# Laying x and v out by piece on the host for the products u = x·v of a long convolution

## Chip, cores and metric

The kernel runs on one core of one Trainium2 chip. The metric is the device time of one execution in microseconds (us); lower is better. Three runs of the kernel before gave a median of 2274.79 us (2274.72 to 2276.05).

## Reference

Two parts follow one another. The first is a long convolution with a gate, for 2 batches of 12480 positions and 128 channels; the second is a dense MLP with a rational function as its activation, over all 24960 positions.

```python
def _attn_ref(x, v, pos_emb, w1, w2):
    B, S, D = x.shape                       # 2, 12480, 128
    h_mlp = np.maximum(pos_emb @ w1, 0.0) @ w2
    window = np.exp(-0.01 * np.arange(S, dtype=np.float32))[:, None]
    h_filt = h_mlp * window
    u = x * v
    L = 2 * S
    Uf = np.fft.rfft(u, n=L, axis=1)
    Hf = np.fft.rfft(h_filt, n=L, axis=0)
    y = np.fft.irfft(Uf * Hf[None, :, :], n=L, axis=1)[:, :S, :]
    return x * y

def _moe_ref(x, w_in, w_out, a, b):         # w_in 128 x 2048, w_out 2048 x 128
    h = x @ w_in
    P = a[0] + a[1] * h + a[2] * h * h + a[3] * h * h * h
    Q = 1.0 + np.abs(b[0]) * np.abs(h) + np.abs(b[1]) * h * h
    return (P / (Q + 1e-06)) @ w_out
```

## The kernel before

The convolution is a Fourier transform in two stages. A position is written as n = 128·m + t: m is the row (98 of them, on the partitions), t the residue (128 of them, in the free dimension). The product u = x·v is therefore kept as tiles of 98 partitions × 32 channels × 128 residues, one for each quarter of the channels; 12480 positions are 97.5 rows of 128, so for residues from 64 on the last row lies behind the end of the sequence and must be zero.

**How u is made.** u comes in pieces: one quarter of the channels (32) by 16 residues. There are 32 pieces a batch. `load_quarter` (L235) loads one piece of x and one of v, through `load_rows` (L133): the tile is 98 partitions × 16 residues × 32 channels, and in DRAM a run of 32 channels is 128 bytes. For residues below 64 that is one transfer for x (L141, 98 rows) and one for v; from 64 on it is two each, 96 full rows (L143) and the short end (L146 for v, with padding; L148 for x). All are issued on SP's queue. `quarter` (L243) makes the tile of u and has POOL set the last two partitions of its upper half to zero (L245). `mult_quarter` (L248) multiplies a piece; it writes u through a turned view, so that neighbouring elements of the output lie 128 floats apart.

**First part** (to about 372 us): the filter's MLP (L494 to L527, 16 tiles in turn), with the weights of the second part converted beside it (`weights_gen`, L450, which loads raw at L323 and L325); then the filter stage from about 82 us on, a loop over 32 groups of four channels in which the transforms of the filter and of batch 0 run: PE (L156, L581, L191 to L194, L588), VectorE (L569 to L577, L174, L175, L206, L207), POOL (L180, L181, L209, L210, L599, L600) and ScalarE. Batch 0's pieces belong to this part, two loaded ahead (`load_u`, L301). Its first eight products run on POOL during the filter's MLP (L559); the other 24 run on VectorE, one in each of the first 24 groups (L641); groups without a product take a step of `weights_gen` instead.

**Second part** (from about 372 us): the MLP, as 208 steps over 52 tiles of positions; L876 to L878 are its first product on PE, L886, L910, L938, L954 and L959 its ScalarE work, L920, L965 and L970 VectorE's, L975 and L981 POOL's, L993 the second product on PE. A list of names with offsets (`FIRST`, `REST`) fixes the order of the instructions on every queue. Into each step go three slots (`slot`, L1021); a slot calls `load_step` (L722) and then takes a piece of the convolution of batch 1 (`conv_step`, L752) or of the inverse transform (L822, L828, L841). `load_step` multiplies on POOL the pieces that have been loaded and issues up to three loads ahead on SP: two products a slot while the first quarter is missing, then one a step. A quarter's products are let in when the transform has come near it. Behind the loads on the same SP queue stand hg (the filter's spectrum for two channels, L709, waited for by VectorE at L202), xt, gt and yc for the inverse transform (L143, L803, L785) and the stores of the output (L1015), in the order of the program; so a load that waits for its buffer holds back what is queued behind it.

Of the kernel before, what the change touches and what calls it, by code (L numbers as in the profile page):

```python
# [9 lines left out]
F32 = mybir.dt.float32  # L10
# [3 lines left out]
ALU = mybir.AluOpType  # L14
# [3 lines left out]
B, S, D = 2, 12480, 128  # L18
FO = 64
DFF = 2048  # L20
N2 = 128
M = 98
# [13 lines left out]
UQ = 32  # L36
UC = 16
NF = DFF // 128
NPT = 5
H2 = N2 // 2  # L40
# [23 lines left out]
def constants():  # L64
    t = np.arange(N2)
    hp = np.arange(N2 // 2)
    m = np.arange(M)
    k1 = np.arange(K1)
    k2 = np.arange(N2)
    f = lambda a: np.ascontiguousarray(a, dtype=np.float32)  # L70
    turn = lambda a, n: 2 * np.pi * (a % n) / n

    def twiddles(ph):
        return f(np.stack([np.concatenate([np.cos(ph)] * 2, 1), np.concatenate([np.sin(ph)] * 2, 1)], 1))

    th = turn(m[:, None] * k1[None, :], N1)
    f1 = f(np.concatenate([np.cos(th), -np.sin(th)], 1))
    tw = twiddles(turn(t[:, None] * k1[None, :], L))

    twh = twiddles(np.tile(turn((2 * hp[:, None] + 1) * k1[None, :], 2 * L), (2, 1)))  # L80
    ps = turn(t[:, None] * k2[None, :], N2)
    dft = f(np.stack([np.cos(ps), np.sin(ps), -np.sin(ps)], 1))
    ph = turn((2 * hp[:, None] + 1) * k2[None, :], 2 * N2)
    ch, sh = np.cos(ph), np.sin(ph)
    dfth = f(np.stack([np.concatenate([ch, sh], 0), np.concatenate([ch, -sh], 0)], 1))
    c, s = ch.T, sh.T
    idfth = f(np.stack([np.concatenate([c, s], 1), np.concatenate([s, c], 1)], 1))
    w = np.where(k1 == 0, 1.0, 2.0) / L
    n2 = np.concatenate([2 * hp + 1, -2 * hp - 1])
    sg = np.where(n2 > 0, 1.0, -1.0)  # L90
    ga = turn(k1[:, None, None] * (2 * N2 * m[None, None, :] + n2[None, :, None]), 2 * L)
    w = w[:, None, None]
    g = f(np.stack([np.cos(ga) * w, -np.sin(ga) * w * sg[None, :, None]], 2))
    win = np.zeros((M * N2,), np.float32)
    win[:S] = WINDOW
    win = win.reshape(M, N2)[:96]
    return {
        "f1": f1,
        "tw": tw,
        "twh": twh,  # L100
        "dft": dft,
        "dfth": dfth,
        "idfth": idfth,
        "g": g,
        "win": f(win),
        "ident": np.eye(128, dtype=np.float32),
    }


@with_exitstack  # L110
def build(ctx: ExitStack, tc, x, v, pos_emb, w1, w2, w_in, w_out, moe_a, moe_b,
          f1_d, tw_d, twh_d, dft_d, dfth_d, idfth_d, g_d, win_d, ident_d, out):
    nc = tc.nc
    ctx.enter_context(tc.manual_schedule())
# [13 lines left out]
    def rows(src, r0, n, t0, k, c0, c):  # L128

        w = src.shape[1]  # L130
        return bass.AP(src.tensor, src.offset + (r0 * N2 + t0) * w + c0, [[N2 * w, n], [w, k], [1, c]])

    def load_rows(dst, src, t0, k, c0, c, pad, queue=nc.sync):  # L133


        h = N2 // 2
        if t0 < h < t0 + k:
            load_rows(dst[:, 0:h - t0], src, t0, h - t0, c0, c, pad, queue)
            load_rows(dst[:, h - t0:k], src, h, t0 + k - h, c0, c, pad, queue)
        elif t0 < h:  # L140
            queue.dma_start(out=dst[0:M], in_=rows(src, 0, M, t0, k, c0, c))  # L141
        else:
            queue.dma_start(out=dst[0:96], in_=rows(src, 0, 96, t0, k, c0, c))  # L143
            if pad:
                a = rows(src, 96, 1, t0, k, c0, c)
                queue.dma_start(out=dst[96:98], in_=bass.AP(a.tensor, a.offset, [[0, 2]] + [list(p) for p in a.ap[1:]]))  # L146
            else:
                queue.dma_start(out=dst[96:97], in_=rows(src, 96, 1, t0, k, c0, c))  # L148

    xb = [x[b] for b in range(B)]  # L150
    vb = [v[b] for b in range(B)]


    def s1_mm(cvt, u, cl0, n, k=M):
# [78 lines left out]
        return pool.tile([K1, 2, N2, CY], F32, tag="ys", name="ys", bufs=1)  # L233

    def load_quarter(pool, b, q, n0, bufs):  # L235
        c0 = q * UQ
        xt = pool.tile([M, UC, UQ], F32, tag="xq", name="xq", bufs=bufs)
        vt = pool.tile([M, UC, UQ], F32, tag="vq", name="vq", bufs=bufs)
        load_rows(xt, xb[b], n0, UC, c0, UQ, False)
        load_rows(vt, vb[b], n0, UC, c0, UQ, True)  # L240
        return xt, vt

    def quarter(pool, name, bufs):  # L243
        u = pool.tile([M, UQ, N2], F32, tag=name[:2], name=name, bufs=bufs)
        nc.gpsimd.memset(u[96:98, :, H2:], 0.0)  # L245
        return u

    def mult_quarter(engine, u, n0, xt, vt):  # L248
        k = M if n0 < H2 else M - 1
        engine.tensor_tensor(  # L250
            out=u[0:k, :, n0:n0 + UC].rearrange("p c t -> p t c"), in0=xt[0:k], in1=vt[0:k], op=ALU.mult)


    wpool = ctx.enter_context(tc.tile_pool(name="wpool", bufs=1))
# [8 lines left out]
    with ExitStack() as st:  # L263
# [30 lines left out]
        for i in range(2):  # L294
            nc.scalar.dma_start(out=bdw2[64 * i:64 * i + 64, :].rearrange("p (s c) -> p s c", s=2),
                              in_=w2.unsqueeze(1).to_broadcast([FO, 2, D]))
# [4 lines left out]
        def load_u():  # L301
            if uload and len(uw) < 2:
                q, n0 = uload.pop(0)
                uw.append((q, n0) + load_quarter(sp, 0, q, n0, 2))

        def mult_u(engine):
            if uw:
                q, n0, xt, vt = uw.pop(0)
                if q not in us:
                    us[q] = quarter(sp, f"hu{q}", 6)  # L310
                mult_quarter(engine, us[q], n0, xt, vt)

        def cvs():
            return spp.tile([128, 2, 512], F32, tag="s", name="cs")
# [290 lines left out]
        for g in range(NG + 3):  # L605
            a = g
            if a < NG:
                zh[a] = ctile(sp, "zh", 2, CG)
                t = cvs()
                s1_mm(t, hf[a // gq], a % gq * CG, CG, MF)  # L610
                s1h_out(t, zh[a])
            a = g - 1
            if 0 <= a < NG:
                hgs[a] = ctile(sp, "hg", 2, CG)
                t = cvs()
# [4 lines left out]
                t = cvs()  # L620
                s1_mm(t, us[a // gq], a % gq * CG, CG)
                s1_out(sp, t, zu[a], CG)
            a = g - 2
            if 0 <= a < NG:
                yy[a] = ctile(sp, "yy", 2, CG)
                t = cvs()
                s2_mm(t, zu.pop(a), CG)
                s2_prod(sp, t, hgs.pop(a), yy[a], CG)
            a = g - 3
            if 0 <= a < NG:  # L630
                if a % 2 == 0:
                    ysd[a // 2] = ystile(sp)
                t = cvs()
                s3p_mm(t, yy.pop(a))
                s3p_out(t, ysd[a // 2], a % 2 * CG, (nc.gpsimd, nc.gpsimd if a < NG - 3 else nc.vector))
                if a % 2 == 1:
                    t = ysd.pop(a // 2)
# [14 lines left out]
    def second_part(short):  # L652
# [69 lines left out]
        def load_step(k=0):  # L722
            for p in us:
                p[2] += p[1] == 0
            for _ in range(2 if not us or us[0][1] else int(k == 0)):
                if coming and (coming[0][0] - 1) * (UQ // CS) <= s1_done[0]:
                    q, n0, xt, vt = coming.pop(0)
                    if q == len(us):
                        us.append([quarter(up, f"uq{q}", 2), N2 // UC, 0])
                    mult_quarter(nc.gpsimd, us[q][0], n0, xt, vt)  # L730
                    us[q][1] -= 1
            while pieces and len(coming) < 3:
                q, n0 = pieces.pop(0)
                coming.append((q, n0) + load_quarter(up, 1, q, n0, 3))
# [345 lines left out]
_INS = ["x", "v", "pos_emb", "w1", "w2", "moe_w_in", "moe_w_out", "moe_a", "moe_b"]  # L1080
_OUTS = [((B * S, D), "float32")]


# [20 lines left out]
```

## Time and profile before

| what | before |
|---|---|
| median of 3 runs | 2274.79 us |
| the profiled execution's own time | 2275.51 us |
| its span in the profile | 2273.6 us |
| PE matmul, PE weight load | busy 89%, 77% |
| VectorE (DVE) | busy 92% |
| ScalarE (ACT) | busy 85% |
| GpSimd (POOL) | busy 90% |
| granted clock of TensorE, mean | 0.981 of full speed |
| DMA packets | 357841, 150.26 MB; under 512 bytes 292518 |
| SP's DMA queue | 124.10 MB, 26.3% of 16 engines' span |

The shares are means over the span; the stages differ, so they tell little of what a change in one stage is worth. The time of the execution is 1.9 us longer than the span. In a timeline a line has the start and the duration in us, the engine, the line of the code, the operation, output and inputs with their sizes, and in brackets how long the engine was idle before and which instruction it had waited for. DVE is VectorE, ACT ScalarE, POOL GpSimd; SPq is SP's instruction queue, on which transfers are issued.

### The profile page before, as it was taken

The page shows a single profiled execution, that of the slowest core. Times are in us where ns is not written, and L with a number is a line of the kernel's source. Part 1 is how long each engine was busy: PE and PEld are TensorE (multiplying, and loading weights), DVE is VectorE, ACT ScalarE, POOL GpSimd, SP SyncE. Part 2 cuts the span into 40 slices and gives each one's busy share as a digit, 9 for nine tenths or more (in the row PEclk, how much of TensorE's full clock was granted, in tenths as well). Part 3 has the DMA queues.
Part 4 walks back from the last instruction along what each step waited for, and adds up shares of the span by engine and source line. Part 5 has one row for each costly group of instructions (what it writes and reads, how often), then busy time and mean ns, then how long its engine had stood idle before and what let it go on. Part 6 is the DMA issues. An engine that isn't in the chain of part 4 may idle for free.

```text
span 2273.6 us, 35833 instructions
## 1 busy us (share of the span) xinstructions
PE 2026.0 (89%) x13344; PEld 1758.5 (77%) x13344; DVE 2083.5 (92%) x2374; ACT 1942.7 (85%) x1971; POOL 2037.5 (90%) x1613
## 2 busy tenths in 40 slices
PE   6899977799999999999999889888888898888887
PEld 3677766688888888888888777777777777777775
DVE  6899995899989997999999889999999999999996
ACT  5422223899989998999999989999999999999996
POOL 4588755999999999899999789999999999999997
PEclk8999998999999999999999999999999999999999
DMA  7456426752155133232122112212112111221100
GB/s 148 113 127 147 117 77 126 118 105 59 46 95 110 43 68 86 62 78 73 53 66 66 46 35 46 42 38 46 32 32 52 31 40 39 48 47 32 36 10 11
DMA packets 357841, 150.26 MB, mean 66 GB/s; under 512 B 292518, under 2 KB 339880, under 8 KB 354776
## 3 DMA queue, kind: packets, MB, share of 16 engines
q1 hardware_dynamic: 350632, 124.10, 26.3%
q10 hardware_dynamic: 7024, 23.76, 3.3%
q8 instruction: 107, 1.75, 0.3%
q14 instruction: 78, 0.64, 0.1%
HBM read 99.65 MB, written 48.17 MB: 65 GB/s over the span
## 4 chain that ended last, share of the span: by engine, by line
POOL 36%; ACT 25%; PE 22%; DVE 10%; issue 3%; DMA 2%; SPq 2%; POOLq 0%; DVEq 0%; ACTq 0%
POOL v L981 19%; POOL v L975 9%; PE acc L993 6%; ACT v L910 6%; ACT l L954 5%; ACT r L959 5%; ACT q L886 4%; POOL q L949 4%; ACT q L938 3%; POOL q L948 2%; PE cv L822 2%; PE cs L588 2%; PE cs L156 2%; PE h L876 2%; PE h L877 2%
## 5 line engine op out<-in xcount | busy, mean ns | idle before, releaser
L981 POOL TENSOR_TENSOR v<-v,q 128x980 f32<-128x980 f32 (+1 forms) x416 | 941.3, 2263 | 49.1 <-DVE q L970 45.7
L993 PE MATMUL acc<-wout,v 128*128 128x128 f32 (+2 forms) x6656 | 843.5, 279 | 113.8 <-POOL v L981 109.0
L993 PEld LDWEIGHTS acc<-wout,v 128*128 128x128 f32 (+2 forms) x6656 | 774.3, 186 | 193.7 <-POOL v L981 168.4
L920 DVE SCALAR_TENSOR_TENSOR v<-v,sc,h 128x980 f32<-128x980 f32 (+1 forms) x416 | 504.7, 1213 | 35.1 <-ACT q L886 29.7
L965 DVE SCALAR_TENSOR_TENSOR q<-q,sc,r 128x980 f32<-128x980 f32 (+1 forms) x416 | 504.6, 1213 | 34.3 <-ACT r L959 33.6
L970 DVE SCALAR_TENSOR_TENSOR q<-q,r 128x980 f32<-128x980 f32 (+1 forms) x416 | 482.0, 1159 | 13.5
L910 ACT ACTIVATE v<-h,sc 128x980 f32<-128x980 f32 (+1 forms) x416 | 438.5, 1084 | 31.6 <-PE h L878 30.3
L959 ACT ACTIVATE r<-l 128x980 f32<-128x980 f32 (+1 forms) x416 | 417.0, 1002 | 9.7 <-DVE q L970 8.9
L975 POOL TENSOR_SCALAR v<-v,sc 128x980 f32<-128x980 f32 (+3 forms) x321 | 422.7, 1317 | 0.0
L954 ACT ACTIVATE l<-q,sc 128x1960 f32<-128x1960 f32 (+1 forms) x208 | 401.3, 1929 | 0.9 <-POOL q L949 0.7
L876 PE MATMUL h<-ahi,win_l 128*128 128x490 f32 (+1 forms) x832 | 360.6, 433 | 29.7 <-DVE v L920 27.2
L877 PE MATMUL h<-alo,win_h 128*128 128x490 f32 (+1 forms) x832 | 319.5, 384 | 0.0
L878 PE MATMUL h<-ahi,win_h 128*128 128x490 f32 (+1 forms) x832 | 317.4, 382 | 0.0
L886 ACT ACTIVATE q<-h 128x980 f32<-128x980 f32 (+1 forms) x303 | 302.6, 999 | 8.9 <-PE h L878 6.2
L876 PEld LDWEIGHTS h<-ahi,win_l 128*128 128x128 f32 x832 | 158.0, 190 | 61.5 <-DVE v L920 37.9
L938 ACT ACTIVATE q<-q,sc 128x1960 f32<-128x1960 f32 (+1 forms) x95 | 185.8, 1955 | 0.0
L878 PEld LDWEIGHTS h<-ahi,win_h 128*128 128x128 f32 x832 | 157.9, 190 | 26.2
L943 ACT ACTIVATE q<-q,sc 128x1470 f32<-128x1470 f32 (+1 forms) x113 | 170.9, 1513 | 0.0
L877 PEld LDWEIGHTS h<-alo,win_h 128*128 128x128 f32 x832 | 158.8, 191 | 13.5 <-DVE alo L847 0.4
L822 PE MATMUL cv<-yc,gt 90*98 90x128 f32 x1004 | 128.2, 274 | 1.5 <-DVE an L828 1.2
L822 PEld LDWEIGHTS cv<-yc,gt 90*98 90x98 f32 x1004 | 118.9, 165 | 13.1 <-DVE an L828 7.5
L949 POOL TENSOR_TENSOR q<-q 128x490 f32<-128x490 f32 (+1 forms) x113 | 111.4, 986 | 9.4
(115 smaller groups left out, 2658.9 us busy)
## 6 DMA issues: line engine op xcount, KB each, us to landing
yc<-y_d SPq DMA_DIRECT2D x23, 900.0 KB
gt<-in_g_dram SPq DMA_DIRECT2D x48, 344.5 KB
h_d<-hg ACTq DMA_DIRECT2D x32, 360.0 KB
y_d<-ys ACTq DMA_DIRECT2D x16, 720.0 KB
hg<-h_d SPq DMA_DIRECT2D x64, 180.0 KB
y_d<-ys SPq DMA_DIRECT2D x16, 720.0 KB
xq<-in_x_dram SPq DMA_DIRECT2D x32, 196.0 KB
vq<-in_v_dram SPq DMA_DIRECT2D x32, 196.0 KB
```

What stands on the lines that cost most here:

```text
L876: nc.tensor.matmul(out=t[:, k, 0:w], lhsT=wl, rhs=hi[:, 0:w], start=True, stop=False)
L877: nc.tensor.matmul(out=t[:, k, 0:w], lhsT=wh, rhs=lo[:, 0:w], start=False, stop=False)
L878: nc.tensor.matmul(out=t[:, k, 0:w], lhsT=wh, rhs=hi[:, 0:w], start=False, stop=True)
L910: nc.scalar.activation(out=v, in_=st_h[s, i], func=AF.Square, bias=col("s"))
L920: stt(out=v, in0=v, scalar=col("k"), in1=h, op0=ALU.add, op1=ALU.mult)
L954: nc.scalar.activation(out=part(st_l, s, i), in_=part(st_q, s, i), func=AF.Ln, **({"bias": col("ka")} if short else {}))
L959: nc.scalar.activation(out=t[:, :, 0:w], in_=halves(st_l[s], i, w), func=AF.Exp, scale=-1.0)
L965: nc.vector.scalar_tensor_tensor(out=q, in0=q, scalar=col("ka") if short else 0.0, in1=st_r[s, i], op0=ALU.add, op1=ALU.mult)
L970: nc.vector.scalar_tensor_tensor(out=q, in0=q, scalar=2.0, in1=st_r.pop((s, i)), op0=ALU.subtract, op1=ALU.mult)
L975: nc.gpsimd.tensor_scalar(out=v, in0=v, scalar1=col("p0" if short else "a0"), scalar2=1.0, op0=ALU.add, op1=ALU.mult)
L981: nc.gpsimd.tensor_tensor(out=v, in0=v, in1=halves(st_q[s], i, w), op=ALU.mult)
L993: nc.tensor.matmul(out=acc[j][0:k, q // 128, :], lhsT=g[:, i, q:q + k], rhs=wout[:, f, :], start=(f == 0 and q == 0), stop=(f == NF - 1), ...
```

## The change

On the host x and v are laid out again, as arrays x_q and v_q with the shape batch, quarter, piece, 98 rows, 32 channels, 16 residues; positions behind the end are zeros. A piece is then contiguous, 98 rows of 2,048 bytes. x itself is still handed over as well, for the gate. The kernel loads a piece of x and one of v with one transfer each; the tiles in SBUF have the channels outside and the residues inside, as u has; the product covers all 98 partitions without a turned view; and the two partitions of u are not set to zero any more. Which engine multiplies, in which order, and how many pieces are loaded ahead stay as they were.

```diff
--- before.py
+++ after.py
@@ -108,7 +108,7 @@
 
 
 @with_exitstack
-def build(ctx: ExitStack, tc, x, v, pos_emb, w1, w2, w_in, w_out, moe_a, moe_b,
+def build(ctx: ExitStack, tc, x, x_q, v_q, pos_emb, w1, w2, w_in, w_out, moe_a, moe_b,
           f1_d, tw_d, twh_d, dft_d, dfth_d, idfth_d, g_d, win_d, ident_d, out):
     nc = tc.nc
     ctx.enter_context(tc.manual_schedule())
@@ -148,7 +148,6 @@
                 queue.dma_start(out=dst[96:97], in_=rows(src, 96, 1, t0, k, c0, c))
 
     xb = [x[b] for b in range(B)]
-    vb = [v[b] for b in range(B)]
 
 
     def s1_mm(cvt, u, cl0, n, k=M):
@@ -233,22 +232,17 @@
         return pool.tile([K1, 2, N2, CY], F32, tag="ys", name="ys", bufs=1)
 
     def load_quarter(pool, b, q, n0, bufs):
-        c0 = q * UQ
-        xt = pool.tile([M, UC, UQ], F32, tag="xq", name="xq", bufs=bufs)
-        vt = pool.tile([M, UC, UQ], F32, tag="vq", name="vq", bufs=bufs)
-        load_rows(xt, xb[b], n0, UC, c0, UQ, False)
-        load_rows(vt, vb[b], n0, UC, c0, UQ, True)
+        xt = pool.tile([M, UQ, UC], F32, tag="xq", name="xq", bufs=bufs)
+        vt = pool.tile([M, UQ, UC], F32, tag="vq", name="vq", bufs=bufs)
+        nc.sync.dma_start(out=xt, in_=x_q[b, q, n0 // UC])
+        nc.sync.dma_start(out=vt, in_=v_q[b, q, n0 // UC])
         return xt, vt
 
     def quarter(pool, name, bufs):
-        u = pool.tile([M, UQ, N2], F32, tag=name[:2], name=name, bufs=bufs)
-        nc.gpsimd.memset(u[96:98, :, H2:], 0.0)
-        return u
+        return pool.tile([M, UQ, N2], F32, tag=name[:2], name=name, bufs=bufs)
 
     def mult_quarter(engine, u, n0, xt, vt):
-        k = M if n0 < H2 else M - 1
-        engine.tensor_tensor(
-            out=u[0:k, :, n0:n0 + UC].rearrange("p c t -> p t c"), in0=xt[0:k], in1=vt[0:k], op=ALU.mult)
+        engine.tensor_tensor(out=u[:, :, n0:n0 + UC], in0=xt, in1=vt, op=ALU.mult)
 
 
     wpool = ctx.enter_context(tc.tile_pool(name="wpool", bufs=1))
@@ -1081,13 +1075,21 @@
 _OUTS = [((B * S, D), "float32")]
 
 
+def by_quarter(x):
+    a = np.zeros((B, M * N2, D), np.float32)
+    a[:, :S] = x
+    a = a.reshape(B, M, N2 // UC, UC, D // UQ, UQ)
+    return a.transpose(0, 4, 2, 1, 5, 3)
+
+
 def kernel(**inputs):
     import concourse.bacc as _bacc
     from concourse.bass_utils import run_bass_kernel_spmd as _run
 
     nc = _bacc.Bacc("TRN2", target_bir_lowering=False, num_devices=1)
     arrays, args = {}, []
-    feeds = [(n, inputs[n]) for n in _INS] + list(constants().items())
+    feeds = [("x", inputs["x"]), ("x_q", by_quarter(inputs["x"])), ("v_q", by_quarter(inputs["v"]))]
+    feeds += [(n, inputs[n]) for n in _INS[2:]] + list(constants().items())
     for name, a in feeds:
         a = np.ascontiguousarray(a)
         if a.dtype == np.float64:
```

## Rows read from the trace of the kernel before

**Rows 1.** The page's first line.

```profile
span 2273.6 us, 35833 instructions
```

**Rows 2.** Windows: us; PE, PEld, DVE, ACT, POOL busy (count); clock, DMA share, GB/s.

```profile
101.25:275.00 173.75, 166.63 (x922) 134.08 (x923) 171.50 (x234) 42.11 (x74) 139.99 (x129) 1.00 0.58 134
330.00:370.00 40.00, 36.14 (x205) 28.73 (x203) 29.40 (x40) 10.92 (x21) 31.04 (x31) 1.00 0.34 108
390.00:420.00 30.00, 17.35 (x99) 14.94 (x98) 19.87 (x19) 23.70 (x22) 23.95 (x15) 0.83 1.07 153
520.00:625.50 105.50, 101.04 (x719) 93.11 (x718) 99.72 (x101) 105.33 (x98) 99.60 (x86) 1.00 0.24 56
625.50:701.40 75.90, 69.87 (x474) 63.80 (x473) 65.26 (x67) 69.20 (x64) 73.27 (x60) 0.96 0.49 94
831.80:904.30 72.50, 66.23 (x453) 58.74 (x452) 59.80 (x65) 62.09 (x64) 71.48 (x65) 0.98 0.48 99
```

**Rows 3.** Timeline of the filter stage with its products: start, us, engine, line, tiles.

```profile
83.31 1.80 POOL L245 MEMSET hu<- 2x2048 f32 x1
...
86.33 1.04 DVE L250 TENSOR_TENSOR hu<-xq,vq 98x512 f32<-98x512 f32 x1
...
199.36 1.11 DVE L250 TENSOR_TENSOR hu<-xq,vq 97x512 f32<-97x512 f32 x1
...
207.53 1.12 DVE L250 TENSOR_TENSOR hu<-xq,vq 97x512 f32<-97x512 f32 x1
```

**Rows 4.** Timeline, VectorE, the same stage once the products are through.

```profile
334.71 0.91 DVE L174 TENSOR_TENSOR ta<-cs,tw 128x720 f32<-128x720 f32 x1
...
338.58 0.91 DVE L569 TENSOR_TENSOR tb<-cs,twh 128x720 f32<-128x720 f32 x1 [0.52 <-POOL zu L181]
...
342.54 0.91 DVE L174 TENSOR_TENSOR ta<-cs,tw 128x720 f32<-128x720 f32 x1
```

**Rows 5.** Waits from 0 to 82 us: us in total, times, longest.

```profile
DVE pw L486 <- DMA pos<-in_pos_emb_dram: 4.3, 3, 2.6
...
DVE i L336 <- DMA raw<-in_moe_w_in_dram: 1.5, 3, 0.8
```

**Rows 6.** Waits from 371 to 440 us, then ScalarE's timeline there.

```profile
POOL uq L250 <- DMA vq<-in_v_dram: 20.9, 6, 13.9
...
413.17 0.99 ACT L886 ACTIVATE q<-h 128x980 f32<-128x980 f32 x1 [2.70 <-POOL v L981]
...
418.64 1.00 ACT L886 ACTIVATE q<-h 128x980 f32<-128x980 f32 x1 [3.60 <-PE h L878]
```

**Rows 7.** Timeline, third and fourth quarter: SP's issues, VectorE's waits behind them.

```profile
640.40 0.33 SPq L803 DMA_DIRECT2D gt<-in_g_dram  x1
...
651.77 1.54 SPq L143 DMA_DIRECT2D xq<-in_x_dram  x1
...
657.01 0.39 SPq L709 DMA_DIRECT2D hg<-h_d  x1
...
660.01 0.91 DVE L202 TENSOR_TENSOR ta<-cv,hg 128x720 f32<-128x720 f32 x1 [4.89 <-DMA hg<-h_d]
...
857.43 0.91 DVE L202 TENSOR_TENSOR ta<-cv,hg 128x720 f32<-128x720 f32 x1 [4.83 <-DMA hg<-h_d]
```

**Rows 8.** Timeline, VectorE in the first microseconds: 256 elements, one element.

```profile
4.28 0.42 DVE L486 TENSOR_TENSOR pw<-pos,ta 82x256 f32<-82x256 f32 x1 [4.28 <-DMA ta<-in_win_dram]
...
10.29 0.16 DVE L370 TENSOR_TENSOR sc<-sc 128x1 f32<-128x1 f32 x1
```

**Rows 9.** Lines by form, POOL, whole span: count, busy us, mean ns, idle before.

```profile
L981 POOL TENSOR_TENSOR v<-v,q 128x980 f32<-128x980 f32 x384 | 881.7, 2297 | 41.9 <-DVE q L970 38.5 <-ACT q L938 3.4
...
L250 POOL TENSOR_TENSOR uq<-xq,vq 98x512 f32<-98x512 f32 x16 | 20.8, 1298 | 17.2 <-DMA vq<-in_v_dram 16.9
...
L245 POOL MEMSET uq<- 2x2048 f32 x4 | 7.2, 1800 | 0.2
```

**Rows 10.** Timeline, POOL, its longest product.

```profile
34.46 3.15 POOL L250 TENSOR_TENSOR hu<-xq,vq 97x512 f32<-97x512 f32 x1
```

## Prediction

> **What bounds the kernel now.** I read the page first, then the windows stage by stage, then the chain of waits and the timelines of the stretches in which x and v are loaded. Of the 2273.6 us of span [rows 1] the loads and products for u lie in the first 905 us; what comes after neither loads nor multiplies them and only moves earlier or later as a whole, because every queue's order is fixed by the program. So the question is which wait ends last in five stretches.
>
> From 101 to 275 us (the filter stage of batch 0) VectorE is busy 171.5 of 173.75 us, POOL 140.0 [rows 2]: VectorE sets the pace. One group of four channels takes 207.53 − 199.36 = 8.17 us while each group carries a product [rows 3], and 342.54 − 334.71 = 7.83 us when the products are through; there VectorE waits 0.52 us before L569 [rows 4]. So without its product VectorE isn't the bound any more: 7.83 us is the floor that other work (PE is busy 36.1 of 40 us there, [rows 2]) sets. Before 82 us VectorE sits idle 4.3 us for pos and 1.5 us for raw [rows 5], transfers that SP issues behind those of x and v. At the start of the second part, POOL waits 20.9 us in six waits for v; ScalarE then stands 2.70 and 3.60 us [rows 6]. In quarters three and four of batch 1 POOL is busy 73.3 of 75.9 and 71.5 of 72.5 us, while the steps between them, without products, are ScalarE's (105.3 of 105.5 us) [rows 2]. In each of the two there is one late filter spectrum: VectorE waits 4.89 and 4.83 us for hg [rows 7], and SP had issued hg only after the four transfers of a piece.
>
> **Part by part.**
>
> *Transfers.* A piece of x and v is now 2 × 98 × 16 rows of 128 bytes, afterwards 2 × 98 rows of 2,048 bytes, with the same 401 kB. From 390 to 420 us, when almost nothing else is moved, the queue shows 153 GB/s at a DMA share of 1.07, so 143 GB/s at a full share; from 330 to 370 us, with rows of some kilobytes, 108 GB/s at 0.34, so 318 [rows 2]. Estimate from these: 2.8 us of all DMA engines a piece now, 1.3 afterwards. Nothing of it is a term by itself; it counts only where somebody waits, below.
>
> *Issues.* SP issues two transfers a piece while n0 < 64 and four above; afterwards always two. One plain issue takes 0.33 us (gt), and the four at 651.77 us, with SP's wait in the first, kept hg back until 657.01 [rows 7]. Two of 0.33 would let hg go some 3.7 us earlier.
>
> *Before 82 us.* Ceiling: the 4.3 + 1.5 us that VectorE waits for pos and raw [rows 5]. Floor: 0, since a pos load waits also for one of three buffers, which VectorE itself frees. I take 3.5, above the middle, because both queues (SP's and the DMA engines') get lighter.
>
> *Products on VectorE (24 of them).* They write u with a step of 512 bytes between neighbours now, afterwards in runs of 16. The first, at 86.33 us, ran with POOL idle (its memset from 83.31 ended at 85.11) and still took 1.04 us; later ones take 1.11 [rows 3]. What would a dense one cost? 256 elements from two SBUF tensors took 0.42 us and one element 0.16 [rows 8]: 0.16 + 511 × 0.26 / 255 = 0.68 us, an estimate. The Trainium skill ("SBUF — State Buffer", section "Door 1: The DMA port swizzle") says that accesses run at full rate while they stay in one 16-byte line and pay at each crossing; by it a step of 512 bytes pays at every element and a run of 16 at every fourth. The trace agrees so far as 1.04 against 0.68 goes. So a product shrinks by 1.11 − 0.68 = 0.43 us; a period of 8.17 − 0.43 = 7.74 lies under the floor of 7.83, so 0.34 a group is what can be had. 24 groups carry one, the first two while the pipeline fills: 22 × 0.34 = 7.5; I take 7.2, because a product still waits a little where POOL is reading. Bounds: 0, and 24 × 0.36 = 8.6.
>
> *Memsets.* Eight of 1.80 us on POOL [rows 9]. The first part's four lie in POOL's slack (34 us between 101 and 275, [rows 2]); if that slack were gone, they'd be 1.8 each. The first one of the second part lies in POOL's wait for v. The other three stand in the POOL-bound bursts and count below.
>
> *Products on POOL.* 32 in the second part, 1298 ns each for 512 elements with the 512-byte step; dense work of POOL's, 980 elements in 2297 ns [rows 9], gives 1200 ns for 512 in proportion. So the step costs POOL 0.1 us at most; I take no change, bounds −0.1 and, upward, the rival below.
>
> *Start of the second part and second quarter.* The first and longest wait (13.9 of the 20.9 us) is covered: POOL's first work on the MLP needs PE, ScalarE and VectorE to go first. What reaches the path is ScalarE's idle time, 2.70 + 3.60 = 6.3 us [rows 6], and one memset of 1.8: ceiling 8.1. I take 5.5; floor 3, if a transfer (yc and gt go first on SP) stays late. Next late there is PE, whose granted clock is 0.83 of its upper level of 2.4 GHz in this stretch [rows 2].
>
> *Third quarter.* The memset's 1.8, and POOL's idle 75.9 − 73.3 = 2.6 that hg caused: 4.4 if POOL then has no idle time at all. I take 4.0; bounds 1.8, and 1.8 + 4.89 = 6.7 if VectorE's whole wait was on the path. *Fourth quarter:* 1.8 + 1.0 = 2.8, I take 2.5, bounds 1.0 and 1.8 + 4.83 = 6.6.
>
> *Sum:* 3.5 + 7.2 + 5.5 + 4.0 + 2.5 = 22.7 us. The profiled execution took 2275.5 us, so 2252.8; the median of the runs is 0.7 below it, so **2252 us**. All floors together give 5.8 (2269 us), all ceilings 35.8 (2239 us).
>
> **Rivals.**
>
> *The products on VectorE don't shrink* (0.16). If what lengthens them is POOL reading SBUF beside them, the layout helps nothing; the sum loses 7.2: 2259 us. For it: they lie between POOL's L181 and L209, and the longer ones exceed the first by 0.07 us. Against it: the first one with POOL idle is almost as long [rows 3]. The Trainium skill (same page, section "Who interferes with whom") has a VectorE instruction with two SBUF inputs contend with a POOL instruction that reads SBUF, which the product is before and after; no row here shows the product dense.
>
> *The loads' waits move instead of going* (0.12). hg also stands behind stores of the output, and the first pieces behind yc. Then 7.2 for VectorE and three memsets of 1.8 remain: 12.6, so 2262 us.
>
> *The transfers aren't what the change says* (0.04): if rows are cut smaller on the way, say to the 64 bytes of one channel, SP and VectorE gain and the DMA engines lose; about 2275 us.
>
> *Slower* (0.03). POOL's product becomes longer, being cut into 32 short rows. The longest product in the trace is one of 3.15 us [rows 10]; 32 × 1.85 = 59 us on an engine that is the bound in the bursts, less 22.7: 2311 us. It decides from 22.7 / 32 = 0.7 us a product upward. Against it: products now write 16 rows of 32 with the largest step and show no cost from it [rows 9].
>
> The forecast itself keeps 0.65.
>
> **How the numbers follow.** 0.2% (4.5 us) is about what can be told from no change here. The forecast and the first two rivals, 0.93 together, lie below 2270; I give 0.02 of that back for several floors at once. Faster 0.91, same 0.05, slower 0.04. The range goes from 2240, near all ceilings, to 2264, past the rival of the loads.
>
> **What the changed profile would show.** Right: xq and vq 64 issues each, 196 kB, none of 2 or 4 kB; L250 on VectorE near 0.7 us, groups 7.8 to 7.9 us apart; no memset of u; hg's waits of 4.8 us gone from VectorE; ScalarE without its two gaps of 2.7 and 3.6 us; POOL's products at 1.3 us; the end 20 us earlier and everything after 905 us of the same length. Wrong: L250 on VectorE still at 1.0 us, or groups stay at 8.17 us because another instruction waits; POOL's wait for v in the second part still 15 us and ScalarE's idle time still there; POOL's product above 2 us.

## The result, and the profile after

The changed kernel took 2254.58 us (median of 5 runs, 2252.79 to 2255.84) beside 2274.79 us for the kernel before in the same series; the ratio is 0.991, with a 95% interval of 0.9899 to 0.992. The interval lies below 1: the kernel is faster by 20.2 us (0.9%), and it ends 2.6 us above the predicted 2252. The profiled execution took 2255.12 us. From the page of the kernel after; the first line answers to [rows 1]:

```profile
span 2253.2 us, 35705 instructions
...
PE 2023.2 (90%) x13344; PEld 1758.5 (78%) x13344; DVE 2073.7 (92%) x2374; ACT 1941.2 (86%) x1971; POOL 2021.5 (90%) x1605
...
DMA packets 169487, 150.31 MB, mean 67 GB/s; under 512 B 91622, under 2 KB 138984, under 8 KB 166424
...
q1 hardware_dynamic: 162280, 124.17, 22.5%
```

The bytes are the same, the packets fewer by half. SP's queue held the DMA engines for 26.3% of 2273.6 us before and 22.5% of 2253.2 now: 598 − 507 = 91 us less, 1.4 us for each of the 64 pieces, about the difference of the prediction's estimates, 2.8 − 1.3.

To see where the time went I cut both traces at the same instructions: VectorE's first of the filter stage (L569 before, L563 after), the second part's first matmul (PE, y and gt), POOL's last product of the second, third and fourth quarters, and VectorE's last copy of a result (128 partitions) for the output, each by its start.

| stage | before, us | after, us | gain | predicted |
|---|---|---|---|---|
| up to the filter stage | 82.36 | 79.55 | 2.8 | 3.5 |
| filter stage | 289.76 | 282.65 | 7.1 | 7.2 |
| start of the second part, second quarter | 110.68 | 106.68 | 4.0 | 5.5 |
| third quarter | 217.34 | 212.42 | 4.9 | 4.0 |
| fourth quarter | 202.91 | 199.76 | 3.2 | 2.5 |
| from there to the last copy | 1361.95 | 1364.04 | −2.1 | 0 |

The first five make 22.0 of the 22.7 us forecast. Then 2.1 us are given back in the part that neither loads nor multiplies x and v.

Windows of the kernel after, with the columns of [rows 2]: the filter stage, the start of the second part, then the product bursts of the third and fourth quarters.

```profile
95.75:266.00 170.25, 168.65 (x937) 136.31 (x936) 167.97 (x238) 42.29 (x74) 133.72 (x129) 1.00 0.43 137
380.00:410.00 30.00, 20.78 (x116) 18.55 (x114) 21.99 (x22) 27.52 (x25) 25.86 (x16) 0.83 0.64 160
...
609.00:683.00 74.00, 70.78 (x506) 64.69 (x505) 68.73 (x70) 73.38 (x68) 73.79 (x61) 1.00 0.37 97
810.90:882.40 71.50, 67.59 (x470) 59.56 (x469) 62.02 (x67) 64.41 (x66) 71.50 (x65) 1.00 0.38 100
```

In the filter stage PE and VectorE are now both within 2.3 us of full. At the start the DMA share is 0.64 where it was 1.07. In the third quarter POOL is idle for 0.2 us where it was idle for 2.6.

Timeline of the kernel after; VectorE's products answer to [rows 3], POOL's L180 is the instruction beside the product, the wait for PE to [rows 6], SP's issues and VectorE's use of hg to [rows 7].

```profile
83.51 0.69 DVE L245 TENSOR_TENSOR hu<-xq,vq 98x512 f32<-98x512 f32 x1
...
199.57 0.83 POOL L180 TENSOR_TENSOR zu<-ta,tb 128x360 f32<-128x360 f32 x1
...
200.20 0.75 DVE L245 TENSOR_TENSOR hu<-xq,vq 98x512 f32<-98x512 f32 x1
...
208.09 0.75 DVE L245 TENSOR_TENSOR hu<-xq,vq 98x512 f32<-98x512 f32 x1
...
404.72 0.99 ACT L880 ACTIVATE q<-h 128x980 f32<-128x980 f32 x1 [2.48 <-PE h L872]
...
633.88 1.83 SPq L237 DMA_DIRECT2D xq<-in_x_q_dram  x1
635.75 0.39 SPq L238 DMA_DIRECT2D vq<-in_v_q_dram  x1
636.19 0.40 SPq L703 DMA_DIRECT2D hg<-h_d  x1
...
640.67 0.91 DVE L201 TENSOR_TENSOR ta<-cv,hg 128x720 f32<-128x720 f32 x1 [0.17 <-POOL v L975]
```

The product fell from 1.11 to 0.75 us and its period from 8.17 to 7.89. Of ScalarE's two gaps at the start one is left, of 2.48 us, and it waits for PE. hg now follows two issues and is there when VectorE comes for it: 0.7 us of waiting for hg in the whole trace, where it was 11.3 in three waits.

Two waits of the kernel after, from 0 to 79.5 us and from 362 to 431; they answer to [rows 5] and [rows 6].

```profile
DVE pw L480 <- DMA pos<-in_pos_emb_dram: 2.1, 2, 1.1
...
POOL uq L245 <- DMA vq<-in_v_q_dram: 15.8, 3, 14.4
```

### The profile page after: what moved, and what is told of

The parts are those of the page before. It is cut to its first block, busy times and chain, and to the rows that moved or that the text cites. A ratio compares the mean times of both kernels' runs of the same rounds, so it can differ in the third digit from the quotient of the medians.

```text
span 2253.2 us, 35705 instructions
## 1 busy us (share of the span) xinstructions
PE 2023.2 (90%) x13344; PEld 1758.5 (78%) x13344; DVE 2073.7 (92%) x2374; ACT 1941.2 (86%) x1971; POOL 2021.5 (90%) x1605
## 3 DMA queue, kind: packets, MB, share of 16 engines
q1 hardware_dynamic: 162280, 124.17, 22.5%
## 4 chain that ended last, share of the span: by engine, by line
ACT 41%; POOL 22%; PE 22%; DVE 7%; issue 5%; DMA 2%; SPq 1%; POOLq 0%; DVEq 0%; ACTq 0%
POOL v L975 10%; ACT v L904 10%; ACT l L948 9%; ACT r L953 9%; PE acc L987 5%; POOL v L969 4%; ACT q L880 4%; ACT q L937 4%; ACT q L932 3%; PE cs L155 3%; PE cs L582 2%; POOL q L943 2%; PE cv L816 2%; PE h L870 1%; PE h L872 1%
## 5 line engine op out<-in xcount | busy, mean ns | idle before, releaser
L975 POOL TENSOR_TENSOR v<-v,q 128x980 f32<-128x980 f32 (+1 forms) x416 | 940.6, 2262 | 52.0 <-DVE q L964 48.7
L880 ACT ACTIVATE q<-h 128x980 f32<-128x980 f32 (+1 forms) x303 | 302.5, 998 | 8.9 <-PE h L872 8.8
```

What stands on the lines that cost most here:

```text
L975: nc.gpsimd.tensor_tensor(out=v, in0=v, in1=halves(st_q[s], i, w), op=ALU.mult)
```

## Experiments

Each edit is against the changed kernel. "Stage" means a row of the table above. "The quarters" are its third to fifth rows, the third with the start of the second part. A run's ratio is to the kernel before on the same chip. A run's time is a median, but its stages come from one profiled execution. With short rows that took 2271.27 us (two issues) and 2272.45 us (four), 5 to 6 us above the medians; with the turned product and the memset 2263.96 us, 2.5 us below.

**The changed kernel once more.** No edit.

> The changed kernel once more, unaltered. The trace of the changed kernel shows 22.0 us gained by 905 us (2.9 before the filter stage, 7.0 in it, 4.0 up to the last product of the second quarter, 4.9 and 3.1 in the third and the fourth) and some 2.1 us lost again later, most of it where batch 0 ends: there TensorE's granted clock is 0.68 in five microseconds in which it was 1.00 before. If that loss belongs to the change, the stretch between the 23rd and the 24th store is 43.8 us here too, and the time is 2254 to 2255. If it is chance, the stretch may be 41 us again and the time 2252. The stages up to 905 us repeat to 0.5 us each in either case.

2255.29 us, ratio 0.9915 (0.9898 to 0.9931). Its stages differ from those of the first profile by 0.6 us up to the filter stage, 0.7 in the filter stage and 0.1 in the quarters. From this one repetition I count as noise what is under 0.3 us in the second part and under 1 us in the filter stage.

**The layout alone undone.**

```diff
-        xt = pool.tile([M, UQ, UC], F32, tag="xq", name="xq", bufs=bufs)
-        vt = pool.tile([M, UQ, UC], F32, tag="vq", name="vq", bufs=bufs)
+        xt = pool.tile([M, UC, UQ], F32, tag="xq", name="xq", bufs=bufs)
+        vt = pool.tile([M, UC, UQ], F32, tag="vq", name="vq", bufs=bufs)
...
-        engine.tensor_tensor(out=u[:, :, n0:n0 + UC], in0=xt, in1=vt, op=ALU.mult)
+        engine.tensor_tensor(
+            out=u[:, :, n0:n0 + UC].rearrange("p c t -> p t c"), in0=xt, in1=vt, op=ALU.mult)
...
-    return a.transpose(0, 4, 2, 1, 5, 3)
+    return a.transpose(0, 4, 2, 1, 3, 5)
```

> The host lays a piece out with the residues outside and the channels inside, 2,048 bytes a row as in the changed kernel and one transfer each; the product again writes u with a step of 512 bytes. So only the layout of the product is undone. If the step is what lengthens VectorE's product: 1.04 us with POOL idle, 1.1 beside it, groups of the filter stage 8.17 us apart, the stage 7 us longer, all other stages as in the changed kernel, 2261 to 2262 us. If POOL's reading beside it was the cause and the lighter transfers took it away: products near 0.75 us and no loss. POOL's products 1.29 to 1.30 us either way.

2260.77 us, ratio 0.9944 (0.9927 to 0.9961). The filter stage is back at 289.43 us; the quarters are 106.56, 213.00 and 199.76, so only the third differs from the change, by 0.6 us, which stays open. The row of the tile hu (durations: ns, least, median, most):

```profile
L245 DVE TENSOR_TENSOR hu<-xq,vq x24: 1023/1108/1122, 83.6 to 269.7; 98x512 f32<-98x512 f32 x24
```

So the stepped writing makes VectorE's product long, 1.02 us with POOL idle, and writing runs of 16 takes 0.34 us off. What POOL adds beside it is the 0.07 us between 0.68 and 0.75 (1.02 and 1.11 when stepped). On POOL the stepping costs next to nothing: its second-part products have means of 1298 ns before [rows 9], 1297 in this run and 1290 after.

**The memset alone back.**

```diff
-        return pool.tile([M, UQ, N2], F32, tag=name[:2], name=name, bufs=bufs)
+        u = pool.tile([M, UQ, N2], F32, tag=name[:2], name=name, bufs=bufs)
+        nc.gpsimd.memset(u[96:98, :, H2:], 0.0)
+        return u
```

> Only the memset of each tile of u is put back, before the products that then write the same elements. If the memsets stood on the path where the prediction put them (second, third and fourth quarter, 1.8 us each, nothing in the filter stage): the stretch up to the last product of the second quarter 1 to 2 us longer, the third and the fourth 1.8 each, the time 4 to 5 us above the changed kernel. If POOL has room for them beside the other engines: under 1 us in all. If the first part isn't POOL's slack after all: another 1.8 each for up to three memsets in the filter stage, so up to 10 us.

2261.06 us, ratio 0.9942 (0.9926 to 0.9959). The third quarter is 1.6 us longer (214.06) and the fourth 2.1 (201.82), the 1.8 of the memset as near as these runs tell. The start with the second quarter is only 0.5 longer (107.14), where 1 to 2 were expected. The filter stage is 1.6 us longer too (284.28), which the prediction had put at nothing. Timeline of this kernel:

```profile
208.60 0.75 DVE L247 TENSOR_TENSOR hu<-xq,vq 98x512 f32<-98x512 f32 x1
...
216.49 1.13 DVE L247 TENSOR_TENSOR hu<-xq,vq 98x512 f32<-98x512 f32 x1
...
224.76 0.74 DVE L247 TENSOR_TENSOR hu<-xq,vq 98x512 f32<-98x512 f32 x1
...
213.58 1.81 POOL L243 MEMSET hu<- 2x2048 f32 x1
215.47 0.82 POOL L179 TENSOR_TENSOR zu<-ta,tb 128x360 f32<-128x360 f32 x1
216.25 0.83 POOL L180 TENSOR_TENSOR zu<-ta,tb 128x360 f32<-128x360 f32 x1
...
223.36 0.82 POOL L179 TENSOR_TENSOR zu<-ta,tb 128x360 f32<-128x360 f32 x1 [1.56 <-DVE tb L174]
```

POOL's idle time comes 1.56 us at a time, one stretch a group, ahead of L179. A memset of 1.81 doesn't fit into it: POOL's next two instructions come late, VectorE's product in that group takes 1.13 instead of 0.75, and the group 224.76 − 216.49 = 8.27 instead of 7.89. The memset of 150.14 us shows the same (a product of 1.12, a group of 8.25); the other two of the first part lie ahead of the steady groups. The rows of the kernel before have it as well:

```profile
155.28 1.80 POOL L245 MEMSET hu<- 2x2048 f32 x1
...
158.21 1.46 DVE L250 TENSOR_TENSOR hu<-xq,vq 98x512 f32<-98x512 f32 x1
```

VectorE's product ends 0.55 us behind the end of POOL's L180, in an ordinary group of the change (200.95 and 200.40 us) as in the one behind the memset (217.62 and 217.08). That fits a product that waits for POOL's instruction: when POOL comes late, the product is long. It needn't be a memset that delays POOL: in the run with four issues below, which has none, one product of 1.09 us at 113.54 ends 0.54 us behind L180, and its group takes 8.23. From the first of the 24 products to the last it is 180.49 us, against 179.79 in the change: 0.7 us. The other 0.9 of the stage lie behind the last product, where two runs of the unedited kernel differ by 0.6; what made them stays open.

**Turned product and memset, long rows.** Both edits above; of the change only the transfers are left.

> The turned product and the memset together, with long rows: only the transfers differ from the kernel before. Theory: a memset in the filter stage costs something only while POOL is near the end of the path there; with the slow product VectorE ends last, so the stage stays at 289.4 to 289.8 us, as in the kernel before (289.76) and with the turned product alone (289.43). Rival: the memset costs 2 us there whatever the product takes, 291.4 us. In the second part the memset costs what it cost alone (0.4, 1.7 and 2.0 us). Time 2264 us by the theory, 2266 by the rival.

2266.47 us, ratio 0.9967 (0.9955 to 0.9978). The filter stage is 289.84 us, which fits the theory to within its spread, yet the theory is wrong. VectorE's timeline:

```profile
213.51 1.10 DVE L247 TENSOR_TENSOR hu<-xq,vq 98x512 f32<-98x512 f32 x1
...
221.66 1.46 DVE L247 TENSOR_TENSOR hu<-xq,vq 98x512 f32<-98x512 f32 x1
...
230.17 1.12 DVE L247 TENSOR_TENSOR hu<-xq,vq 98x512 f32<-98x512 f32 x1
```

Here too the product that follows a memset is 0.36 us longer and its group takes 8.51 instead of 8.16. A memset in the filter stage thus costs 0.35 to 0.38 us whichever way the product writes, not 2, and isn't hidden either. In the second part the costs add up as expected: third and fourth quarters of 214.17 and 201.81 us. Against the kernel before, the third quarter is 3.2 us shorter through the transfers alone, the fourth 1.1, the start with the second quarter 4.4.

**Short rows, two issues.** The host cuts every 2,048-byte row into 16 pieces of 128 bytes that lie 256 bytes apart.

```diff
-        nc.sync.dma_start(out=xt, in_=x_q[b, q, n0 // UC])
-        nc.sync.dma_start(out=vt, in_=v_q[b, q, n0 // UC])
+        for t, src in ((xt, x_q), (vt, v_q)):
+            nc.sync.dma_start(out=t.rearrange("p (g h) t -> p g (h t)", g=16), in_=src[b, q, n0 // UC][:, :, 0:32])
...
```

> The transfers are cut into rows of 128 bytes again (the host leaves a gap of 128 bytes behind every 128), with one transfer each for x and v and the product as in the changed kernel. If the bytes a row matter for the waits, the stretch before 82 us is some 3 us longer and the start of the second part with the second quarter some 3 to 4, while the third and the fourth quarter, in which hg stood behind the number of issues, lose under 1 us each: 2260 to 2262 us. If the number of issues is what counts everywhere: no stage loses more than 1 us, 2255 to 2256.

2265.47 us, ratio 0.9958 (0.9945 to 0.997), more than the 2260 to 2262 expected. It takes 83.69 us up to the filter stage and 110.97, 217.71 and 200.99 in the quarters. By the medians 10.2 us are lost against the change once more, on the same chip. That is nearly what the transfers alone had gained (in the run above the five stages are 11.7 us shorter than before), and with two issues. The five stages of this profiled execution lose 15.4, more than the median. That the third and fourth quarter would lose under 1 us was a miss. Timeline of this kernel, SP's queue, then VectorE:

```profile
648.37 1.64 SPq L238 DMA_DIRECT2D xq<-in_x_q_dram  x1
650.06 2.52 SPq L238 DMA_DIRECT2D vq<-in_v_q_dram  x1
652.63 1.12 SPq L703 DMA_DIRECT2D hg<-h_d  x1
...
656.45 0.91 DVE L201 TENSOR_TENSOR ta<-cv,hg 128x720 f32<-128x720 f32 x1 [3.23 <-DMA hg<-h_d]
```

The tile xq shows every issue of it, first in the kernel after, then with short rows, then in the kernel before (98, 96 and one row of 16 pieces):

```profile
L237 SPq DMA_DIRECT2D xq<-in_x_q_dram x64: 316/317/1840, 6.6 to 853.9; - x64
```

```profile
L238 SPq DMA_DIRECT2D xq<-in_x_q_dram x64: 824/842/3022, 6.6 to 868.4; - x64
```

```profile
L141 SPq DMA_DIRECT2D xq<-in_x_dram x32: 317/330/2632, 6.4 to 835.0; - x32
L143 SPq DMA_DIRECT2D xq<-in_x_dram x32: 312/316/1608, 23.3 to 875.1; - x32
L148 SPq DMA_DIRECT2D xq<-in_x_dram x32: 516/731/2556, 23.7 to 875.5; - x32
```

With long rows an issue of xq occupies SP for 0.32 us, with short ones in this run for 0.84, and that of vq here for 2.52. hg goes later and is waited for 3.23 us. But the number of rows doesn't set the time of an issue by itself: in the kernel before, x in 1,568 short rows takes SP 0.33 us (L141), and the 16 rows behind 1,536 others (L148) 0.73, at the place of [rows 7] even 2.39 us. What sets it stays open.

**Long rows, four issues.** Rows 0 to 95 and 96 to 97 are transferred separately for residues from 64, as before.

```diff
-        nc.sync.dma_start(out=xt, in_=x_q[b, q, n0 // UC])
-        nc.sync.dma_start(out=vt, in_=v_q[b, q, n0 // UC])
+        for t, src in ((xt, x_q), (vt, v_q)):
+            for r0, r1 in ((0, M),) if n0 < H2 else ((0, 96), (96, M)):
+                nc.sync.dma_start(out=t[r0:r1], in_=src[b, q, n0 // UC][r0:r1])
```

> Pieces with residues from 64 on are loaded with two transfers for x and two for v again (96 rows and 2 rows), of 2,048 bytes a row; all else as in the changed kernel. If hg in the third and the fourth quarter was late because of the issues in front of it: VectorE waits for hg again, some 1 to 4 us in each, those stretches 1 to 3 us longer, the other stages within 1 us; 2256 to 2260 us. If the size of the rows decides (a transfer of long rows is taken over faster by the queue): under 1 us in all.

2253.8 us, ratio 0.9903 (0.9884 to 0.9922): no stage is longer (106.52, 212.52 and 199.76 us in the quarters). Timeline:

```profile
634.04 1.91 SPq L239 DMA_DIRECT2D xq<-in_x_q_dram  x2
635.99 0.64 SPq L239 DMA_DIRECT2D vq<-in_v_q_dram  x2
636.99 0.39 SPq L704 DMA_DIRECT2D hg<-h_d  x1
...
640.90 0.91 DVE L201 TENSOR_TENSOR ta<-cv,hg 128x720 f32<-128x720 f32 x1 [0.39 <-DMA hg<-h_d]
```

Two issues more move hg by 0.8 us, from 636.19 to 636.99, and VectorE then waits 0.39 us for it, where it waited 0.17 for POOL.

**Both together.** The two edits above; this is nearly how the kernel before loads (there the short rows of a piece begin 512 bytes apart in DRAM, here 256).

> Both together: rows of 128 bytes and four transfers for pieces with residues from 64 on, so the transfers of the kernel before, with the dense product and no memset. If the transfers and the product are separate causes that add up, everything but the filter stage and the memsets is lost again: about 2.9 before 82 us, 3 in the start and second quarter, 3 and 1.3 in the third and the fourth, so 2263 to 2266 us, hg late by 4 to 5 us in each of the two. If the product's gain in the filter stage depended on the lighter transfers, that stage is longer than 284 us as well.

2267.44 us, ratio 0.9964 (0.9952 to 0.9976), with 110.61, 217.88 and 201.34 us in the quarters: as with short rows alone. The ratio's interval overlaps with that of short rows and two issues, so the number of issues adds nothing that these runs tell.

**One transfer a piece.** The host puts x and v side by side, 98 rows of 4,096 bytes, into one tile.

```diff
...
+        t = pool.tile([M, 2, UQ, UC], F32, tag="xq", name="xq", bufs=bufs)
+        nc.sync.dma_start(out=t, in_=x_q[b, q, n0 // UC])
+        return t[:, 0], t[:, 1]
...
```

> The change carried one step further: x and v of a piece lie side by side in DRAM and come with one transfer of 4,096 bytes a row, so one issue a piece instead of two. If issues on SP still hold something up, the stretch before 82 us and the start of the second part gain 0.5 to 2 us together: 2252 to 2254 us. If what was to be had there is spent, the time stays that of the changed kernel within 0.5 us in every stage.

2256.49 us, ratio 0.9913 (0.9894 to 0.9931): nothing gained, none of the first five stages shorter by 0.3 us. From 2,048-byte rows and two issues on, one issue less and rows twice as long shorten nothing more.

**Half of the second part's products on VectorE.**

```diff
-                    mult_quarter(nc.gpsimd, us[q][0], n0, xt, vt)
+                    mult_quarter(nc.vector if q and n0 // UC % 2 else nc.gpsimd, us[q][0], n0, xt, vt)
```

> A version that may be faster: in the second part every second product of quarters two to four runs on VectorE instead of POOL. In the changed kernel POOL is busy 73.8 of 74.0 us in the third quarter but ScalarE 73.4 too, and 71.5 of 71.5 in the fourth where ScalarE has 64.4 and PE 67.6. If POOL alone is the bound in the fourth: 2 to 4 us less there, nothing in the third, 2250 to 2253 us. If VectorE's product beside POOL's reading costs both engines (the lock between them), the quarters get longer: 2255 to 2260.

2273.09 us, ratio 0.9983 (0.9971 to 0.9996): all but 2 us of the gain is gone, where at most 2260 us was expected. The third and fourth quarters take 220.22 and 209.56 us. The row of the tile uq shows what VectorE's twelve products took:

```profile
L245 DVE TENSOR_TENSOR uq<-xq,vq x12: 685/2304/6456, 408.1 to 898.5; 98x512 f32<-98x512 f32 x12
```

The shortest is as short as in the filter stage, the median three times that, the longest 6.46 us. Up to the last product of the second quarter it looked 3.3 us shorter (103.42), and so I tried that quarter alone.

**Four products of the second quarter on VectorE.** As above with `q == 1` in place of `q`.

> Every second product of the second quarter alone (four of them) goes to VectorE, the third and fourth quarters stay on POOL as in the changed kernel. Theory: the start with the second quarter is 3 us shorter, as in the run with half the products on VectorE (103.4 us against 106.7), the third and fourth quarters keep 212.4 and 199.8 us: 2251 to 2252 us beside the changed kernel's 2254 to 2255. Rival: what VectorE takes on is given back in the third quarter (its stage then 3 us longer, or more), and the time is 2254 us or more.

2259.14 us, ratio 0.9937 (0.9923 to 0.9951), slower than the change; the rival was right, and the loss greater than it said. The gain had been one of the mark: products on another queue come earlier, the steps of the MLP don't. By the same ScalarE instruction (L880) in both traces, this kernel is 1.9 us ahead at 400 us, 0.1 ahead at 459 and 5.5 behind at 488. Timeline:

```profile
463.54 4.49 POOL L975 TENSOR_TENSOR v<-v,q 128x980 f32<-128x980 f32 x2
...
463.66 4.92 DVE L245 TENSOR_TENSOR uq<-xq,vq 98x512 f32<-98x512 f32 x1
...
470.61 0.64 PE L835 MATMUL cv<-ident,an 98*128 98x98 f32 x5 [2.70 <-DVE ta L201]
...
472.99 0.99 ACT L953 ACTIVATE r<-l 128x980 f32<-128x980 f32 x1 [3.93 <-DVE q L964]
```

VectorE's product began 0.12 us behind two of POOL's and ended 0.55 us behind their end, after 4.92 us; the first of the four went the same way (4.87 us from 402.98, POOL's pair from 402.78 to 407.30). Its end too lies 0.55 us behind that of the pair, the distance that the filter stage's product keeps to L180. The other two met no pair and took 0.69 and 0.76. Behind the long one PE stood still for 2.70 us and ScalarE for 3.93, and TensorE's granted clock was 0.66 of 2.4 GHz from 470 to 480 us, against 1.00 in the ten before. The Trainium skill ("SBUF — State Buffer", section "Who interferes with whom") says that a VectorE instruction with two SBUF inputs and a GpSimd instruction that reads SBUF exclude one another through a shared port; the two long products agree, at 4.9 against 0.7 us. None of the versions tried is faster than the change by more than its own runs differ.

## What was given back after 905 us

"Everything after 905 us of the same length" failed by 2.1 us. The place is where the order of the instructions goes over from `FIRST` to `REST` (step 95 of the MLP), while the inverse transform changes from batch 0 to batch 1. Between the 23rd and the 24th copy of a result (VectorE, `ot` from `acc`, 128 partitions) lie 41.11 us before and 43.77 after, 2.66 more. In the kernel after:

```profile
1274.20 0.55 DVE L998 COPY ot<-acc 128x384 f32<-128x384 f32 x1
...
1317.97 0.56 DVE L998 COPY ot<-acc 128x384 f32<-128x384 f32 x1 [0.78 <-PE acc L987]
```

Two windows of each kernel, from 8.4 to 18.4 us behind the earlier copy (1296.65 us before, 1274.20 after); first the kernel before, then the kernel after:

```profile
1305.00:1310.00 5.00, 4.03 (x21) 3.83 (x22) 3.72 (x4) 1.82 (x2) 4.39 (x3) 0.66 0.63 135
1310.00:1315.00 5.00, 5.00 (x36) 4.60 (x34) 2.56 (x3) 3.13 (x4) 3.72 (x2) 1.00 0.00 0
```

```profile
1282.60:1287.60 5.00, 3.43 (x19) 3.10 (x20) 3.67 (x4) 1.81 (x3) 4.33 (x3) 0.64 0.61 133
1287.60:1292.60 5.00, 5.00 (x24) 4.73 (x24) 2.41 (x2) 1.35 (x2) 3.76 (x2) 0.68 0.00 0
```

In both kernels the granted clock falls to about 0.65 there, PE having been idle for some of the stretch. Before, it is back at 1.00 in the next five microseconds and PE does 36 matmuls; after, its mean there is 0.68, the first three of the five microseconds at 0.50, the lower level of 1.2 GHz, and PE does 24. What differs is when the clock falls. In windows of 2 us counted from the earlier copy, the change has 1.00 up to 8 us and 0.50 from 10 to 16; the run with four issues, whose piece is 41.49 us long, has 0.70 already from 6 to 8, 0.50 from 8 to 12, and 1.00 again from 14 on. The twelve profiles have two values for this piece: 41.1 to 41.9 us in seven (before, layout undone, layout undone with memset, four issues, one transfer, both with products on VectorE) and 43.8 to 43.9 in five (the change, its repetition, the memset, both with short rows). The dense layout, the memset, the short rows and the four issues each occur on both sides, so no part of the change decides it alone; what decides when the clock falls stays open.

## Why the prediction was right, and where its steps were not

The forecast held, and its sum came within 0.7 us of what was gained up to 905 us. That close it came by luck: the start gave 1.5 us less than forecast, the third and fourth quarters together 1.6 more. Its terms:

- **Before 82 us**, 3.5: measured 2.8. VectorE's waits for pos fell from 4.3 to 2.1 us. With short rows it is lost (83.69 us), so it is the transfers', as said.
- **Products on VectorE**, 7.2: measured 7.1 in the stage, 7.0 from the first of the 24 products to the last, yet made up otherwise. The layout gave 0.28 a group instead of 0.34, 23 × (8.165 − 7.89) = 6.3, since the product beside POOL took 0.75 and not 0.68 (which was right with POOL idle), and VectorE still sets the pace at 7.89 instead of giving way to a floor of 7.83. The missing 0.7 came from the two memsets. The 0.68 was worked out from contiguous rows, so for the crossings within a run of 16 that the prediction names no price shows.
- **First part's memsets "lie in POOL's slack"**: this step failed. The 34 us of slack were a sum over a window; in the memset's run one stretch of it is 1.56 us, shorter than one memset of 1.80. The kernel before shows the price, a product of 1.46 us at 158.21, which wasn't read. At 0.32 to 0.38 us each, for two of the four, it changed little.
- **Start and second quarter**, 5.5: measured 4.0, above the floor of 3. PE is what is late next, as said: ScalarE's remaining gap of 2.48 us waits for it, and its granted clock is still 0.83. The memset, 1.8 in the ceiling, was worth 0.5. Of a sign of being wrong that the prediction names, half came: POOL still waits 15.8 us for v. Most of that is one wait of 14.4 us, the one that the prediction had called covered; the other half, ScalarE's idle time, went from 6.3 us to the one gap.
- **Third and fourth quarters**, 4.0 and 2.5: measured 4.9 and 3.2. The memset gave 1.6 and 2.1 of it. The transfers alone gave 3.2 and 1.1 (product and memset undone), more than the 2.2 and 0.7 left for them in the forecast; that all of it came through hg is not shown.
- **"Issues"**: the effect came, the cause was wrong. hg was not late because four issues stood ahead of it on SP: four issues of long rows delay it by 0.8 us and lengthen no stage, and two issues of short rows bring the waits back (9.0 us in three for hg). Nor does every issue take the 0.33 us of gt, which the prediction used for all: at the place of [rows 7] the four took 1.54, 2.39, 0.58 and 0.55. From xq's issue to hg's it was 5.24 us before and is 2.31 after, 2.9 less; the forecast was 3.7, which by its own rows should be 3.3, since the first of two issues keeps its 1.54. The lateness is SP's and not the landing's: from the end of hg's issue to VectorE's start it is 2.6 us before, 2.7 with short rows and 3.5 with four issues of long ones.
- **Products on POOL**, no change: right, 1298 against 1290 ns.

Of the rivals, *the products don't shrink* falls by the run with the layout undone; *the loads' waits move* falls by the two quarters, where hg is in time; *the transfers aren't what the change says* by the packets and by 64 issues each of xq and vq; *slower* by POOL's 1290 ns. What was missing altogether was that a later part could change with the clock, by 2.7 us; the change and its repetition both have the longer value, so whether it is chance stays open.

## What to carry to other kernels

Slack of an engine counts by the single gap: a short instruction put into an engine with 20% idle time still costs when it is longer than one gap. Count the rows of a transfer and not only the transfers: here short rows held the issuing queue, and what stood behind them came late. And compare stages by instructions whose engine and order are the same in both kernels, for a mark that was itself moved shows gains that aren't there.

## What was not expected of the hardware

- Short rows hold SP's queue longer than more issues do: from xq's issue to hg's it is 2.31 us with two issues of long rows, 2.95 with four, 4.26 with two of short rows. A single issue doesn't last by its own rows: 1,568 took 0.33 or 0.84 us, 16 behind 1,536 others up to 2.56.
- A VectorE product of two SBUF tensors that starts just behind a pair of POOL's waits both of them out: 4.9 us instead of 0.7. In the filter stage too it ends 0.55 us behind POOL's instruction.
- A 512-byte step of the output costs VectorE 0.34 us on 512 elements and POOL 0.02 at most.
- The same piece of program takes 41.1 to 41.9 or 43.8 us, with the place in it at which the granted clock of TensorE falls.
